# Two of the five VectorE steps of a weight conversion, given to ScalarE and GpSimd for fourteen pieces

## The chip, the core and the metric

The kernel runs on one core of one Trainium2 chip. A core has TensorE (PE in the profile, with its weight loads as PEld), VectorE (DVE), ScalarE (ACT), GpSimd (POOL) and SyncE (SP), whose queue issues most of the DMAs. Each engine works through its own queue in order, and engines wait for each other by semaphores. The metric is the device time of one execution in microseconds (us), as a median over runs.

## The reference, cut to what matters

An attention with decay runs over 4 batches, 8 heads, 768 positions and 64 channels a head. Its result, laid side by side over the heads, is x with 512 columns. Then comes a mixing by two Fourier transforms, a normalization, and two matrix products with a ReLU between them:

```python
X = np.fft.fft(np.fft.fft(x, axis=1), axis=2)
u = x + np.real(X).astype(np.float32)
un = (u - mean(u)) / np.sqrt(var(u) + 1e-06)
ch = np.maximum(un @ w_ch1, 0.0) @ w_ch2      # 512x2048 and 2048x512
return (u + ch).astype(np.float32)
```

The inputs q, k, v are float32. The two weight matrices arrive as float64, since they are float32 numbers multiplied by a float64 scalar. TensorE works on float32 here, so the kernel turns each weight, two 32-bit words in memory, into one float32.

## The kernel before, in words

The attention (`attn`, lines from 300 on) goes batch by batch, and in each batch over 6 chunks of 128 positions. A chunk loads k, q and v (L303), transposes k and q on TensorE (L314, L319), copies the transposes out of PSUM on ScalarE (kT at L316, qT at L321), and multiplies them (L338). VectorE multiplies the scores with the decay (sc, L343, two instructions a chunk, which read PSUM) and the transposed q with powers of the decay (qs, L325, which reads PSUM too). GpSimd makes the decayed k (kd, L310) and decays the running state (L362), to which VectorE adds (L363). TensorE makes the new state (L358) and the output (L373, L379), which ScalarE copies out (oT, L382) and TensorE turns back (L395). The Fourier part of a batch (`fft_ln`) begins with folds on VectorE (L476 to L571) and goes on with matrix products (L603, L615 to L620), sums and statistics (L691 to L695, L634, L635) and a normalization (L655). The `mlp` makes the two products with the weights (L749, L763). From 260 us on most of the time goes into these products, in a form that trades products for sums of quarter matrices.

The conversion of weights is `load_weights`. The weights are cut into NW = 32 word pieces of 128 partitions by 512 values. A piece comes as `raw`, 128 x 1024 words, whose even words are the low halves (`lo`) and whose odd words are the high halves (`hi`) of the numbers. Two ScalarE and five VectorE instructions make the float32:

- ScalarE L225: the sign, from the top 16 bits, as bf16, into one half of a small buffer `e`.
- VectorE L226: the exponent's bits are masked out, into the other half of `e`; ScalarE L228: they become the exponent of a bf16.
- VectorE L230: the upper mantissa with a leading one, as an integer, into the destination `w`.
- VectorE L232: the lower word scaled by 2 to the -32 and added.
- VectorE L234: exponent times sign, both bf16; VectorE L235: the mantissa, scaled, times that.

`raw` has 4 buffers (tag "hr", which the mlp uses as well), `e` has 2. In the order of pieces, two quarters of the first half of the weights (8 pieces of the first matrix, then 8 of the second) come first. A generator (`weights`) yields between pieces with a cost, and `weave` interleaves it with the attention by these costs: 8 pieces beside batch 0's attention, 6 beside batch 1's, the rest later. The framework then orders each engine's queue by its own estimates, except where `keep_in_program_order` pins an instruction. For the first two pieces (`late_words`) and for pieces 3 to 8 (`held_back`) some of the steps are pinned.

Of the kernel before, what the change touches and what calls it, by code (L numbers as in the profile page):

```python
# [11 lines left out]
F32 = mybir.dt.float32  # L12
# [4 lines left out]
AF = mybir.ActivationFunctionType  # L17
ALU = mybir.AluOpType
# [59 lines left out]
def kernel(  # L78
# [10 lines left out]
    nc = tc.nc  # L89
# [105 lines left out]
    NW = 2 * KO * DFF // WP  # L195
# [8 lines left out]
    def load_weights(dst, src):  # L204

        if src.dtype == F32:
            nc.sync.dma_start(dst, src)
            yield 1.0
            return
        raw = hp_.tile([128, 2 * WP], U32, tag="hr", name=f"raw{cnt[0]}")  # L210
        e = ep.tile([128, 2 * WP], U16, tag="e", name=f"e{cnt[0]}")
        pw, sg = e[:, 0:WP], e[:, WP:2 * WP].bitcast(BF16)
        cnt[0] += 1
        nc.sync.dma_start(raw, src.bitcast(U32))
        if LAG[0] <= landed[0] < LAG[1]:
            yield 0.5
        lo, hi = raw[:, 0:2 * WP:2], raw[:, 1:2 * WP:2]
        top = raw.bitcast(U16)[:, 3:4 * WP:4]
        d = dst.bitcast(U32)


        held_back = LAG[0] <= landed[0] < LAG[1]
        landed[0] += 1
        pin = tc.keep_in_program_order if late_words else lambda i: i
        pin(nc.scalar.activation(sg, top.bitcast(I16), AF.Sign))  # L225
        first_step = nc.vector.tensor_scalar(pw, top, 0x7FF0, None, op0=ALU.bitwise_and)  # L226
        (tc.keep_in_program_order if held_back else pin)(first_step)
        nc.scalar.activation(pw, pw, AF.Relu, bias=cvt[:, 0:1], scale=8.0)  # L228
        (tc.keep_in_program_order if held_back else pin)(
            nc.vector.tensor_scalar(d, hi, 0x000FFFFF, 0x00100000, op0=ALU.bitwise_and, op1=ALU.bitwise_or))  # L230
        del late_words[0:1]
        nc.vector.scalar_tensor_tensor(dst, lo, 2.0 ** -32, d, op0=ALU.mult, op1=ALU.add)  # L232
        p = pw.bitcast(BF16)
        nc.vector.tensor_tensor(p, p, sg, op=ALU.mult)  # L234
        nc.vector.scalar_tensor_tensor(dst, dst, 2.0 ** -20, p, op0=ALU.mult, op1=ALU.mult)  # L235
        yield 0.5 if held_back else 1.0

    late_words, landed, LAG = [0, 1], [0], (2, NW // 4)

    def weights():  # L240

        for h in range(2):
            for f in range(h * DFF // 2, (h + 1) * DFF // 2, WP):
                for c in range(KO):
                    yield from load_weights(w1[:, c, f:f + WP], w1v[:, c, f:f + WP])
            for c in range(h * FO // 2, (h + 1) * FO // 2):
                yield from load_weights(w2[:, c, :], w2v[:, c, :])
# [1172 lines left out]
```

## Time and profile before

| What | Value |
|---|---|
| median of 3 runs | 777.14 us (776.51 to 780.37) |
| profiled execution | 774.72 us, of which the span shown is 772.9 us |
| PE busy | 752.0 us, 97% |
| DVE busy | 602.9 us, 78%, 1167 instructions |
| ACT busy | 230.5 us, 30%, 532 instructions |
| POOL busy | 177.6 us, 23%, 202 instructions |
| L235, 32 instructions | median 689 ns, 658 to 1556 |
| L232, 32 instructions | median 684 ns, 671 to 694 |
| L225 and L228, 32 each | median 683 and 722 ns |

The profile is of one execution. A row of a group names the line, the engine, the operation, and what is written and read. A row of the timeline gives the start in us, the duration in us, and in brackets how long the engine had been idle before it and what ended that. Where the text says "the chain", it is the chain of work that ended last. Shares over the whole span hide the stages: the fourteen pieces of the change are converted in the first 125 us, while the attention runs.

### The profile page before, as it was taken

The numbers are of one execution on the slowest core, as the hardware profiler recorded it, in microseconds if no ns is written. First come the engines' busy times: TensorE is split into PE (matmuls) and PEld (weight loads), VectorE is DVE, ScalarE is ACT, GpSimd is POOL, SyncE is SP. The second block draws the span as 40 slices with busy tenths as digits, with TensorE's granted clock in tenths as the row PEclk, the third lists the DMA queues.
The fourth block names the chain that finished last, engine by engine and source line by source line (L and its number), as shares of the span: only waits on it lengthen the run. The fifth ranks groups of instructions, "written<-read, shape, count | busy, mean of one in ns | idle before, by whom it ended". The sixth has DMA issues, their size and how long they took to land.

```text
span 772.9 us, 14999 instructions
## 1 busy us (share of the span) xinstructions
PE 752.0 (97%) x5784; PEld 646.6 (84%) x5784; DVE 602.9 (78%) x1167; ACT 230.5 (30%) x532; POOL 177.6 (23%) x202
## 2 busy tenths in 40 slices
PE   6889999999999999999999999999999999999997
PEld 5778877767685967769846889999999999999997
DVE  6999999774936585336898999788986699758983
ACT  3755444424531221422101221034301342024310
POOL 3223330010112113220005951360015001230013
PEclk9999999999999999999999999999999999999999
DMA  9988732236843148731333465776545456455442
GB/s 236 257 176 245 202 125 94 97 93 169 249 119 95 50 82 251 185 104 40 110 68 116 153 222 158 276 233 201 185 124 178 125 180 187 125 176 179 139 140 77
DMA packets 152957, 120.23 MB, mean 156 GB/s; under 512 B 114238, under 2 KB 114622, under 8 KB 152886
## 3 DMA queue, kind: packets, MB, share of 16 engines
q1 hardware_dynamic: 145824, 100.51, 46.5%
q0 software_dynamic: 4032, 12.99, 4.9%
q10 hardware_dynamic: 3030, 5.78, 2.1%
q8 instruction: 46, 0.75, 0.4%
q14 instruction: 25, 0.20, 0.1%
HBM read 88.04 MB, written 31.20 MB: 154 GB/s over the span
## 4 chain that ended last, share of the span: by engine, by line
PE 82%; DVE 10%; DMA 3%; issue 1%; ACT 1%; SPq 1%; POOL 1%; DVEq 0%; ACTq 0%; POOLq 0%
PE p L1181 21%; PE p L1107 17%; PE pm L749 13%; PE pm L763 9%; PE p L1023 6%; PE pa L603 3%; PE pa L338 3%; PE pa L379 2%; PE pa L373 2%; PE pa L314 1%; PE pa L358 1%; PE pa L395 1%; PE pa L763 1%; DMA raw<-in_moe_w_ch_dram 1%; PE pa L319 1%
## 5 line engine op out<-in xcount | busy, mean ns | idle before, releaser
L749 PE MATMUL pm<-ut,w 128*128 128x256 f32 x512 | 118.3, 381 | 0.0
L763 PE MATMUL pm<-w,hr 128*128 128x512 f32 x240 | 109.0, 596 | 0.1
L749 PEld LDWEIGHTS pm<-ut,w 128*128 128x128 f32 x512 | 94.7, 190 | 14.4 <-issue 2.7
L763 PEld LDWEIGHTS pm<-w,hr 128*128 128x128 f32 x240 | 43.6, 190 | 44.5 <-issue 42.8
L1202 POOL TENSOR_TENSOR y<-y,u 128x512 f32<-128x512 f32 x12 | 19.9, 1662 | 186.8 <-DVE y L1211 155.5
L1181 PE MATMUL p<-tx,sx 128*128 128x128 f32 x400 | 52.7, 275 | 0.0
L1181 PEld LDWEIGHTS p<-tx,sx 128*128 128x128 f32 x400 | 48.6, 192 | 0.0
L1116 DVE TENSOR_TENSOR ha<-p,ha 128x512 f32<-128x512 f32 x60 | 39.9, 683 | 8.5 <-PE p L1107 8.3
L1187 ACT COPY y<-p 128x128 f32<-128x128 f32 x48 | 12.8, 266 | 103.6 <-PE p L1181 103.1
L310 POOL TENSOR_TENSOR kd<-k,decay 128x512 f32<-128x512 f32 x20 | 21.4, 1071 | 88.5 <-PE pa L358 47.4
L343 DVE TENSOR_TENSOR sc<-pa,decay 128x512 f32<-128x512 f32 x48 | 30.9, 682 | 12.5 <-PE pa L338 12.3
L1189 DVE TENSOR_TENSOR y<-p,y 128x128 f32<-128x128 f32 x92 | 25.5, 284 | 16.1 <-PE p L1181 9.4
L1181 PE MATMUL p<-w,ha 128*128 128x128 f32 x288 | 37.4, 275 | 0.0
L1116 DVE TENSOR_TENSOR hs<-p,hs 128x512 f32<-128x512 f32 x39 | 26.1, 683 | 12.4 <-PE p L1107 12.4
L338 PEld LDWEIGHTS pa<-qT,kT 64*128 64x128 f32 x384 | 25.1, 193 | 12.2 <-ACT qT L321 6.4
L1181 PEld LDWEIGHTS p<-w,ha 128*128 128x128 f32 x288 | 34.9, 192 | 0.1
L1107 PE MATMUL p<-sx,tx 128*128 128x128 f32 x264 | 33.9, 275 | 0.0
L757 ACT ACTIVATE hr<-pm 128x256 f32<-128x256 f32 x44 | 16.7, 383 | 57.5 <-PE pm L749 53.5
L638 POOL TENSOR_SCALAR ve<-mv 128x2 f32<-128x2 f32 x12 | 5.9, 491 | 120.1 <-DVE mv L635 120.1
L338 PE MATMUL pa<-qT,kT 64*128 64x128 f32 x384 | 30.1, 292 | 2.9 <-ACT qT L321 2.9
L1107 PEld LDWEIGHTS p<-sx,tx 128*128 128x128 f32 x264 | 31.6, 192 | 0.0
L379 PE MATMUL pa<-sc,v 128*64 128x128 f32 x384 | 28.6, 282 | 1.1 <-DVE sc L343 1.1
(274 smaller groups left out, 1747.5 us busy)
## 6 DMA issues: line engine op xcount, KB each, us to landing
tx<-td SPq DMA_DIRECT2D x84, 256.0 KB, 2.8
raw<-in_moe_w_ch_dram SPq DMA_DIRECT2D x32, 512.0 KB, 5.2
tx<-sd SPq DMA_DIRECT2D x63, 256.0 KB, 2.8
k<-in_k_dram SPq DMA_DIRECT2D x24, 256.0 KB, 5.2
q<-in_q_dram SPq DMA_DIRECT2D x24, 256.0 KB, 5.9
v<-in_v_dram SPq DMA_DIRECT2D x24, 256.0 KB, 4.9
td<-tx SPq DMA_DIRECT2D x21, 256.0 KB, 2.0
ud<-x SPq DMA_DIRECT2D x16, 256.0 KB, 2.3
```

The source lines that it names most:

```text
L310: nc.gpsimd.tensor_tensor(kd, kt, kpow, op=ALU.mult)
L338: mm(pss[hi][:, hp, :], lhsT=kT[HD[hi], hp, :], rhs=qT[HD[hi], hp, :], start=True, stop=True)
L343: nc.vector.tensor_tensor(t, pss[hi], decay[:, hi::2, :], op=ALU.mult)
L379: mm(po[HD[hi], hp, :], lhsT=vt[:, 2 * hp + hi, :], rhs=sc[hi][:, hp, :], start=(c == 0 and hp == 0), stop=(hp == HP - 1), skip_group_chec ...
L603: mm = nc.tensor.matmul(ps[:, n, :], lhsT=piece(a, i, n), rhs=cs[0:rows, a, i in (2, 3), n, :], start=(a == 0), stop=(a == 1))
L749: nc.tensor.matmul(ps, lhsT=w1[:, c, 128 * fc:128 * fc + 128], rhs=ut[:, c, :], start=(c == 0), stop=(c == KO - 1))
L763: return nc.tensor.matmul(ps, lhsT=hr[(fc - f0) // 4][:, fc % 4, 128 * i:128 * i + 128], rhs=w2[:, fc, :], start=(fc == f0), stop=(fc == f ...
L1023: nc.tensor.matmul(ps, lhsT=s2.A[a][:, kt, 128 * i:128 * i + 128], rhs=U[b][:, kt, :], start=(first and kt == 0), stop=(kt == 1), skip_gro ...
L1107: nc.tensor.matmul(ps[:, 128 * i:128 * i + 128], lhsT=ab[m][0][:, 128 * i:128 * i + 128], rhs=ab[m][1], start=(start and i == 0), stop=Tru ...
L1116: V.tensor_tensor(o, p, o, op=ADD)
L1181: nc.tensor.matmul(ps[:, 0:HM // 2], lhsT=ab[m][0][i], rhs=ab[m][1][:, i, :], start=(start and i == 0), stop=(i == HF // 2 - 1), skip_grou ...
L1189: V.tensor_tensor(o, ps[:, 0:HM // 2], o, op=ADD)
```

## The change

A new flag `shared` holds for the third to the sixteenth piece (indices 2 to 15). For them ScalarE scales the lower words by 2 to the -52 and writes them back as float32 into the places where they were read. VectorE's first sum then takes the mantissa integer, scales it by 2 to the -20 and adds the scaled lower word, in one instruction. The product with sign and exponent is left, as a plain product, to GpSimd. Exponent times sign stays on VectorE. The other 18 pieces are converted as before. The program has one VectorE instruction less, one ScalarE and one GpSimd instruction more for each of the fourteen pieces.

```diff
         held_back = LAG[0] <= landed[0] < LAG[1]
+        shared = LAG[0] <= landed[0] < NW // 2
...
-        nc.vector.scalar_tensor_tensor(dst, lo, 2.0 ** -32, d, op0=ALU.mult, op1=ALU.add)
         p = pw.bitcast(BF16)
-        nc.vector.tensor_tensor(p, p, sg, op=ALU.mult)
-        nc.vector.scalar_tensor_tensor(dst, dst, 2.0 ** -20, p, op0=ALU.mult, op1=ALU.mult)
+        if shared:
+
+            low = lo.bitcast(F32)
+            nc.scalar.activation(low, lo, AF.Copy, scale=2.0 ** -52)
+            nc.vector.scalar_tensor_tensor(dst, d, 2.0 ** -20, low, op0=ALU.mult, op1=ALU.add)
+            nc.vector.tensor_tensor(p, p, sg, op=ALU.mult)
+            nc.gpsimd.tensor_tensor(dst, dst, p, op=ALU.mult)
+        else:
+            nc.vector.scalar_tensor_tensor(dst, lo, 2.0 ** -32, d, op0=ALU.mult, op1=ALU.add)
+            nc.vector.tensor_tensor(p, p, sg, op=ALU.mult)
+            nc.vector.scalar_tensor_tensor(dst, dst, 2.0 ** -20, p, op0=ALU.mult, op1=ALU.mult)
```

## The prediction

> **What bounds the kernel now.** I read first the stretches of the span (busy time of each engine in each), because the change touches only word pieces 3 to 16, which are converted between 24 and 125 us. Columns: stretch, length, busy us (and instructions) of PE, weight load, DVE, ACT, POOL, the clock, the DMA share, GB/s.
>
> ```profile
> 20.00:30.00 10.00, 9.18 (x125) 7.68 (x123) 9.67 (x17) 8.37 (x20) 3.04 (x3) 1.00 1.04 264
> 30.00:40.00 10.00, 8.68 (x116) 7.39 (x115) 9.69 (x19) 6.26 (x15) 1.99 (x2) 1.00 1.03 251
> 40.00:50.00 10.00, 8.56 (x94) 7.23 (x94) 9.68 (x19) 8.57 (x22) 1.06 (x1) 1.00 0.98 214
> 70.00:80.00 10.00, 9.83 (x82) 8.91 (x79) 9.57 (x23) 7.32 (x16) 3.27 (x2) 1.00 0.97 267
> 80.00:90.00 10.00, 9.19 (x114) 7.78 (x114) 10.00 (x21) 4.86 (x12) 2.54 (x4) 1.00 0.59 143
> 95.00:112.00 17.00, 17.00 (x84) 14.27 (x83) 15.22 (x39) 7.43 (x19) 8.27 (x8) 1.00 0.53 174
> ```
>
> VectorE is the fullest engine until 90 us, and ScalarE is near full from 20 to 30 and 40 to 50. From 95 to 140 us TensorE has no gap (28.00 busy of 28 in the stretch after the last one shown), so nothing that VectorE saves there shows. Over 11 to 90 us the ten-microsecond stretches give TensorE 7.3 us of idle time in sum: that is all a gain can come from. Next, TensorE's instructions in order of time, whose brackets tell which engine ended each gap:
>
> ```profile
> 34.56 0.66 PE L395 MATMUL pa<-ident,ds 128*128 128x128 f32 x4 [1.32 <-ACT ds L388]
> 42.25 1.64 PE L338 MATMUL pa<-qT,kT 64*128 64x128 f32 x16 [0.52 <-ACT qT L321]
> 48.53 0.66 PE L395 MATMUL pa<-ident,ds 128*128 128x128 f32 x4 [0.92 <-ACT ds L442]
> 51.86 0.40 PE L379 MATMUL pa<-sc,v 128*64 128x128 f32 x2 [0.97 <-DVE sc L343]
> 88.59 1.09 PE L373 MATMUL pa<-qs,st 64*64 64x128 f32 x16 [0.53 <-DVE qs L325]
> ```
>
> Only two of these gaps, 0.97 and 0.53 us, are VectorE's. A third, 1.32 us, is VectorE's at one remove (ACT L228 waited 0.90 us for the mask L226, and the copy L388 was queued behind it). The others are ScalarE's own. So about 2.8 us of idle time can shrink with a faster VectorE; the other 4.5 us can't, and ScalarE gets work. Last, the collisions of VectorE and GpSimd:
>
> ```profile
> 57.11 1.06 POOL L310 TENSOR_TENSOR kd<-k,decay 128x512 f32<-128x512 f32 x1 [2.12 <-issue]
> 71.80 2.89 POOL L362 TENSOR_TENSOR st<-sd,qpow 128x256 f32<-128x256 f32 x1 [1.42 <-PE pa L379]
> 81.94 1.06 POOL L310 TENSOR_TENSOR kd<-k,decay 128x512 f32<-128x512 f32 x1 [7.25 <-PE pa L358]
> 82.30 1.24 DVE L235 SCALAR_TENSOR_TENSOR w<-w,e 128x512 f32<-128x512 f32 x1
> ```
>
> L235 takes 0.68 us alone and 1.24 beside kd: it really began at 83.54 - 0.68 = 82.86, which is 0.92 after kd did. The fold at 63.35 gives 0.94 in the same way. So a GpSimd product of this size holds VectorE up for about 0.93 us from its start. Beside the kd at 57.11 the two sc of L343, which read PSUM, took their usual 1.28: such work is not held up. The third line is the reverse: with VectorE's instructions back to back, the small product (0.67 elsewhere) needed 2.89 us and ended only after VectorE paused at 74.2.
>
> [...]
>
> **The change part by part.** I walk through the instructions as the changed program orders them. TensorE's and SP's orders are unchanged; no DMA is added, and the raw buffer is released by the instruction that stands where L232 stood.
>
> *Removed:* L235 for 14 pieces. Starts around it are 0.60 us apart (78.56 to 79.17), so 14 x 0.60 = 8.4 us of VectorE. *Replaced one for one:* L232 by the new sum, the same kind of instruction on the same shape, 0.68: nothing.
>
> *Added on ScalarE:* 14 scalings [...]mostly in its pauses, but in order ahead of copies that TensorE waits for. *Added on GpSimd:* 14 products; the kd row gives 1.06, the y row at L1202 gives 1.66 when disturbed; I take 1.06, of which 0.93 blocks VectorE unless it runs PSUM work or idles. *New wait:* the small buffer e (two of them) is released by GpSimd's product instead of L235. The mask on VectorE and the sign on ScalarE of the next piece but one wait for it, with everything queued behind them. *On GpSimd's queue* kd, the state decay L362 and the statistics stand behind products. That is covered: kd of 30.67 is used by L358 at 37.10, the decay of 32.48 at 39.48, some 6 us each.
>
> *24 to 44 us, pieces 3 to 7.* VectorE isn't what holds the chunks here: qs at 27.79 begins when ACT qT ends, and sc at 37.00 and 43.72 wait 0.24 and 0.15 us for TensorE. What VectorE saves is lost in those waits. Product by product the lock costs about 0, 0.7, 0.45, 0.74 and 0. The 1.32 us gap gets some 0.3 shorter; but piece 7's L228 is now queued ahead of kT and a scaling comes before it, which sets L338 at 42.25 back by about 0.2 from where it was. Sum +0.1, bounds -1.3 (the whole gap) and +1.0.
>
> *44 to 52 us, piece 8 and the first folds.* From sc at 43.72 to sc at 51.03 VectorE is unbroken, and TensorE waits for the latter. Less 0.60. The product starts under fold L476, and L477 waits for L476's result (48.10 follows 48.06), so GpSimd gets in there: +0.93. And the program now places two more folds, L480 (0.33) and L476 (0.60), ahead of this sc: +0.93. Sum +1.26, I take +1.2; if the product misses that slot +0.3; at best -0.75, when L338 ends (50.28). Between 52 and 62 VectorE has slack (0.65 at 54.5, 0.52 at 62.1), and the delay goes through with TensorE.
>
> *62 to 89 us, pieces 9 to 13.* VectorE is unbroken from sc at 62.14 to qs at 87.88, except for 0.36 at 74.2, and TensorE waits for that qs. Less 4 x 0.60 = 2.4 (piece 13's L235 stood behind qs). Piece 13's L234 comes ahead of it: +0.34. Piece 11's mask is placed right behind piece 10's and needs piece 9's product, which is queued behind the decay of 71.80 that starves: VectorE stops for 0.5 + 0.95, of which 0.36 it lost before: +1.1. Products of pieces 10 and 12 fall among masks: 2 x 0.93. Piece 11's falls beside sc: 0. Piece 13's beside L691 and L692, which read PSUM: +0.3. Sum -2.4 + 0.34 + 1.1 + 1.86 + 0.3 = +1.2; bounds -0.5 (the idle time to be had) and +2.5.
>
> *After 95 us.* Pieces 14 to 16 lie beside a gapless TensorE: 0, which costs up to 1 us if GpSimd gets the statistics out late.
>
> Sum: 0.1 + 1.2 + 1.2 = +2.5 us. On the profiled execution's own 774.72 us (span 772.9) that is 777.2. The median of the runs shown, 777.14, lies 2.4 above that execution; added to the median it is 779.6, which I predict.
>
> **The rivals.**
> *Faster.* The products mostly fall beside PSUM work and idle moments, and VectorE's 97% is the true bound. Then the three gaps go (1.32 + 0.97 + 0.53 = 2.8), and with less head-of-line waiting on ScalarE some more, up to the 7.3 us: 774.3, at the extreme 769.8. For it speaks the busy share; against it, that VectorE waits for others at each chunk until 44 us and that the kd collisions are no rarity.
> *Clearly slower.* One mechanism: the lock costs more than it saves. If all 14 products meet SBUF work, each costs 0.93 - 0.60 = 0.33, 4.6 us; with the two folds ahead of sc (0.93) and the stop for piece 11 (0.5 beyond the lock) that is +6.0: 783.1. It takes the lead where the mean block exceeds 0.60 us also from 24 to 44 us, so that sc stops waiting for TensorE there. My walk has a mean of 0.54 over the first 11 products.
> *Nothing.* The chunks go at the pace of TensorE, ScalarE and the loads (DMA share 0.98 to 1.04 from 20 to 50 us), and what moves on VectorE is absorbed: 777.1 within 1 us.
>
> **How the numbers follow.** Chances: the forecast 0.35 (its own range 777.5 to 781.5), faster 0.33, clearly slower 0.22, nothing 0.10. About 0.5%, 3.9 us, is what a measurement of this kernel can tell from no change. Of faster, 0.20 lies beyond it, since that needs more than the three gaps; of the slower cases 0.22 + 0.06. The rest, 0.52, is within. The range runs from 772.0 (5.1 us of the 7.3) to 783.5 (just past the slower rival); about 0.1 is left out on either side.
>
> **What would show it.** In the changed profile: L235's rows down from 32 to 18; VectorE's mask, sum and fold rows with mean durations up by some tenths; the product on GpSimd at 1.1 to 1.4; sc of the second sequence's first chunk near 52.3 in place of 51.03; a VectorE gap ended by POOL before a mask near 75; qs later than 87.88 by about 2.5. If sc there starts before 51 us, or VectorE's rows stay at their means, I am wrong.

## The result, and the profile after

The changed kernel takes 787.62 us (median of 6 runs, 785.02 to 792.56), the kernel before 777.44 us (6 runs, 775.66 to 780.37). The ratio is 1.0134, with a 95% interval from 1.0114 to 1.0153: 10.2 us slower, where 2.5 us slower had been forecast, and outside the range. The profiled execution took 786.97 us, its span is 785.2 us against 772.9.

The busy times are the first surprise. Part 1 of the page of after:

```profile
PE 754.4 (96%) x5784; PEld 647.5 (82%) x5784; DVE 603.5 (77%) x1153; ACT 238.3 (30%) x546; POOL 196.4 (25%) x216
```

VectorE has 14 instructions fewer and is as busy as before (602.9 us). What was taken away came back as collisions: an instruction that is kept out by GpSimd counts as busy while it waits (the fold L486 below is busy for 1.53 us beside a product instead of 0.69; E15 to E18 separate the two). The groups of after on VectorE, shapes kept apart (busy us, mean ns | idle before):

```profile
L227 DVE TENSOR_SCALAR e<-raw 128x512 uint16<-128x512 uint16 x32 | 17.9, 558 | 7.1 <-DMA raw<-in_moe_w_ch_dram 5.5 <-POOL w L240 1.6
L231 DVE TENSOR_SCALAR w<-raw 128x512 uint32<-128x512 uint32 x32 | 16.0, 501 | 0.0
L238 DVE SCALAR_TENSOR_TENSOR w<-w,raw 128x512 f32<-128x512 uint32 x14 | 10.9, 775 | 0.7 <-ACT raw L237 0.2
```

The same three steps had means of 461, 444 and 685 ns before. Lines from 245 on of before are 9 further down in after; the sign L225 is L226, the mask L226 is L227, the exponent L228 is L229, the relu of the mlp L757 is L766, sc L343 is L352, qs L325 is L334. The files of the experiments have line numbers of their own; there the names of the tiles tell what a row is.

TensorE, which up to 140 us had only two waits for VectorE of more than 0.2 us, 0.97 and 0.53 us, has longer ones now. TensorE's rows of after with the large waits:

```profile
54.86 0.40 PE L388 MATMUL pa<-sc,v 128*64 128x128 f32 x2 [2.08 <-DVE sc L352]
...
95.88 1.09 PE L382 MATMUL pa<-qs,st 64*64 64x128 f32 x16 [1.95 <-DVE qs L334]
...
142.15 3.66 PE L758 MATMUL pm<-ut,w 128*128 128x256 f32 x8 [2.40 <-ACT hr L766]
```

The first two answer to the waits of 0.97 and 0.53 us at 51.86 and 88.59 of before. The third has no counterpart: before, TensorE had no gap from 95 to 140 us. And its eight matmuls take 3.66 us, where eight of this kind take 1.89 elsewhere in the trace. The stretches of after show why (the clock is the third column from the right):

```profile
140.00:142.00 2.00, 0.00 (x0) 0.00 (x0) 1.50 (x4) 1.45 (x3) 0.00 (x0) 1.00 0.67 233
142.00:144.00 2.00, 1.85 (x5) 1.50 (x6) 2.00 (x6) 0.86 (x3) 0.00 (x0) 0.58 0.07 29
144.00:146.00 2.00, 2.00 (x8) 1.64 (x7) 2.00 (x6) 1.60 (x5) 0.00 (x0) 0.57 0.39 111
```

After the idle time TensorE's granted clock is at half for some 3.4 us (0.65, 0.50, 0.50 and 0.64 in the four microseconds from 142 us on).

The way the delay builds up is best seen from the starts of the same TensorE step in both traces, since TensorE's order is the same. Worked out as after less before; E1, E4, E13 and E16 are experiments below (an offset of up to some 2 us comes from the loads at 27 us, which differ from execution to execution: TensorE waits 1.78 us for one in E1 and 2.34 in E13):

| TensorE step, start before | after | E1 | E4 | E13 | E16 |
|---|---|---|---|---|---|
| L338 at 27.87 | +1.26 | +1.25 | +1.24 | +2.24 | +0.44 |
| L338 at 49.12 | +1.88 | +1.09 | +1.40 | +1.93 | -0.04 |
| L338 at 55.19 | +3.00 | +1.34 | +2.52 | +4.21 | -0.46 |
| L338 at 60.95 | +3.34 | +1.34 | +2.86 | +4.75 | -0.46 |
| L338 at 86.90 | +5.87 | +1.75 | +5.12 | +4.74 | +0.00 |
| L373 (qs) at 88.59 | +7.29 | +3.28 | +7.37 | +6.91 | -0.40 |
| L660 (un) at 92.08 | +7.30 | +3.28 | +8.95 | +8.44 | -0.39 |
| L660 at 150.53 | +11.65 | +4.27 | +9.49 | +8.44 | -0.39 |

Three stages lose: 49 to 61 us, 61 to 92 us, and 121 to 150 us. In the first, VectorE's rows of after show both predicted losses, the collision and the two folds that now stand ahead of sc:

```profile
49.33 1.53 DVE L486 TENSOR_TENSOR fo<-fo,xn 128x512 f32<-128x512 f32 x1
...
53.10 0.41 DVE L489 TENSOR_TENSOR fo<-fo 65x255 f32<-65x255 f32 x1
53.43 0.68 DVE L485 TENSOR_TENSOR fe<-x,x 128x512 f32<-128x512 f32 x1
54.03 1.28 DVE L352 TENSOR_TENSOR sc<-pa,decay 128x512 f32<-128x512 f32 x2
```

L486 takes 1.53 instead of 0.69 us beside a product, and sc begins at 54.03 instead of 51.03. In the second stage VectorE's rows of after have the predicted stop of piece 11's mask for GpSimd:

```profile
79.32 0.43 DVE L227 TENSOR_SCALAR e<-raw 128x512 uint16<-128x512 uint16 x1 [1.64 <-POOL w L240]
```

The third stage shows at ScalarE. Its rows of after:

```profile
132.58 0.57 ACT L673 COPY ut<-pa 128x512 f32<-128x512 f32 x1
137.93 0.70 ACT L226 ACTIVATE e<-raw 128x512 bf16<-128x512 int16 x1 [4.79 <-DMA raw<-in_moe_w_ch_dram]
138.50 0.74 ACT L229 ACTIVATE e<-e,cvt 128x512 uint16<-128x512 uint16 x1
140.55 0.67 ACT L226 ACTIVATE e<-raw 128x512 bf16<-128x512 int16 x1 [1.31 <-DMA raw<-in_moe_w_ch_dram]
141.12 0.70 ACT L229 ACTIVATE e<-e,cvt 128x512 uint16<-128x512 uint16 x1
141.74 0.36 ACT L766 ACTIVATE hr<-pm 128x256 f32<-128x256 f32 x1
```

The relu for which TensorE waits is queued behind two pieces (the 18th and 19th) that wait for their loads. These pieces are not among the fourteen. Before, this relu stood behind the sign of the first, which didn't wait for its load, and ahead of the sign of the second, which did. The change doesn't touch it: the scheduler, which orders each engine's queue, placed it otherwise once the instructions around it were others. ScalarE's order alone doesn't make this wait: in E14, which has it with VectorE's order of before, the delay is 6.12 us at the step before this one and 6.13 us behind it.

### The profile page after: what moved, and what is told of

Same layout as the page of the kernel before. It is cut to its first block, busy times and chain, and to the rows that moved or that the text cites. A ratio compares the mean times of both kernels' runs of the same rounds, so it can differ in the third digit from the quotient of the medians.

```text
span 785.2 us, 15030 instructions
## 1 busy us (share of the span) xinstructions
PE 754.4 (96%) x5784; PEld 647.5 (82%) x5784; DVE 603.5 (77%) x1153; ACT 238.3 (30%) x546; POOL 196.4 (25%) x216
## 4 chain that ended last, share of the span: by engine, by line
PE 81%; DVE 10%; DMA 4%; ACT 2%; issue 2%; POOL 1%; SPq 1%; DVEq 0%; ACTq 0%; POOLq 0%
PE p L1190 21%; PE p L1116 17%; PE pm L758 12%; PE pm L772 9%; PE p L1032 6%; PE pa L347 3%; PE pa L388 2%; PE pa L612 2%; PE pa L382 2%; DMA raw<-in_moe_w_ch_dram 2%; PE pa L323 1%; PE pa L367 1%; PE pa L404 1%; DMA q<-in_q_dram 1%; PE pa L328 1%
## 5 line engine op out<-in xcount | busy, mean ns | idle before, releaser
L758 PE MATMUL pm<-ut,w 128*128 128x256 f32 x512 | 120.1, 385 | 2.4 <-ACT hr L766 2.4
L352 DVE TENSOR_TENSOR sc<-pa,decay 128x512 f32<-128x512 f32 x48 | 30.9, 682 | 13.1 <-PE pa L347 13.1
L766 ACT ACTIVATE hr<-pm 128x256 f32<-128x256 f32 x44 | 16.8, 384 | 56.9 <-PE pm L758 54.0
```

Source lines behind the costliest of these rows:

```text
L352: nc.vector.tensor_tensor(t, pss[hi], decay[:, hi::2, :], op=ALU.mult)
L758: nc.tensor.matmul(ps, lhsT=w1[:, c, 128 * fc:128 * fc + 128], rhs=ut[:, c, :], start=(c == 0), stop=(c == KO - 1))
```

## The experiments

Three theories were to be told apart. The lock: GpSimd's products exclude VectorE, as forecast, only more of it. ScalarE: the scalings stand ahead of copies that TensorE waits for. The order: the loss comes from where the scheduler put other instructions, not from the work that was moved.

The summary first; "V" and "S" are the orders of VectorE's and ScalarE's other instructions. Ratios are to before, run on the same chip beside each kernel; medians of different rows can come from different chips, so the text compares ratios.

| | work | order | median us | ratio, 95% interval |
|---|---|---|---|---|
| after | both | new V, new S | 787.62 | 1.0134 (1.0114 to 1.0153) |
| E1 | both | old V, old S | 780.48 | 1.0043 (1.0030 to 1.0056) |
| E2 | scaling | old V, old S | 777.10 | 1.0001 (0.9989 to 1.0014) |
| E3 | product | old V, old S | 780.40 | 1.0040 (1.0025 to 1.0056) |
| E4 | both | new V, old S | 785.49 | 1.0102 (1.0074 to 1.0129) |
| E5 | both | old V, new S | 781.26 | 1.0070 (1.0048 to 1.0093) |
| E6 | none | V of after | 782.79 | 1.0101 (1.0074 to 1.0128) |
| E7 | none | S of after | 780.87 | 1.0077 (1.0051 to 1.0104) |
| E8 | product, pieces 9 to 16 | old V, old S | 778.97 | 1.0029 (1.0011 to 1.0047) |
| E9 | both | after, hr moved | 785.79 | 1.0118 (1.0093 to 1.0143) |
| E10 | both | after, qs moved | 787.25 | 1.0139 (1.0108 to 1.0171) |
| E11 | both | E1, qs moved | 779.93 | 1.0034 (1.0019 to 1.0049) |
| E12 | none | before, qs moved | 776.75 | 1.0001 (0.9986 to 1.0016) |
| E13 | none | V of after, old S | 781.45 | 1.0075 (1.0037 to 1.0114) |
| E14 | none | old V, S of after | 781.31 | 1.0051 (1.0036 to 1.0066) |
| E15 | no product at all | old V, old S | 775.10 | 0.9973 (0.9964 to 0.9983) |
| E16 | memset of w for it | old V, old S | 774.68 | 0.9970 (0.9952 to 0.9988) |
| E17 | square of w for it | old V, old S | 779.56 | 1.0030 (1.0009 to 1.0051) |
| E18 | memset of e for it | old V, old S | 775.21 | 0.9986 (0.9972 to 1.0000) |

### Work and order apart: E1 to E5

An order is held by an edge, without a semaphore, from each instruction of an engine to the next one in the wanted order; added instructions are left free.

```diff
+    for x, y in zip(line, line[1:]):
+        tc.add_manual_dep(y, x.name, mybir.DependencyInfo(
+            mybir.DependencyClass.NoSync, mybir.DependencyReason.DATA), reason="as_before")
```

E1 is the change with VectorE's and ScalarE's orders of before.

> The change's work whole (14 scalings on ScalarE, 14 products on GpSimd), but ScalarE's and VectorE's other instructions stand in the order that they had before the change. The order theory (the loss comes from what the scheduler rearranged: relu hr behind two pieces' loads at 137 us, two folds ahead of sc) expects within 3 us of before, 777 to 780. The lock theory (GpSimd's products hold VectorE up) expects 782 to 785: only the 4.35 us at 137 to 142 us and some 1 us for the folds come back. The ScalarE theory (the scalings are in the way of copies that TensorE waits for) expects the same total, but with gaps ended by ScalarE copies, not by sc and qs.

E1 is 0.43% over before, some 3.3 us, of after's 1.34%. So two thirds of the loss are order, and the order theory's number is met. What is left sits where the lock theory has it. TensorE's two large waits in E1:

```profile
53.20 0.40 PE L482 MATMUL pa<-sc,v 128*64 128x128 f32 x2 [1.22 <-DVE sc L446]
...
91.87 1.09 PE L476 MATMUL pa<-qs,st 64*64 64x128 f32 x16 [2.05 <-DVE qs L428]
```

The first is the 0.97 us of before with 0.25 on it, not 2.08 as in after: the two folds no longer stand ahead. The second has grown by 1.5 us although nothing new stands ahead of qs.

E2 keeps the scaling on ScalarE and leaves the product to VectorE:

```diff
-            nc.gpsimd.tensor_tensor(dst, dst, p, op=ALU.mult)
+            nc.vector.tensor_tensor(dst, dst, p, op=ALU.mult)
```

> Only the scaling on ScalarE; the last product stays on VectorE, so VectorE does as many instructions as before and GpSimd no more than before; orders as before the change. The ScalarE theory expects 780 to 783 (3 us or more over before). The lock theory expects 777 to 778.5: ScalarE has pauses. The order theory expects 777 to 778.

The ratio is 1.0001. The ScalarE theory falls: fourteen scalings of 0.69 us (median of the row in after) cost nothing that can be measured in this order.

E3 moves the product alone; the factor goes into the bias of the exponent's conversion:

```diff
-        nc.scalar.activation(pw, pw, AF.Relu, bias=cvt[:, 0:1], scale=8.0)
+        nc.scalar.activation(pw, pw, AF.Relu, bias=(cvt20 if shared else cvt)[:, 0:1], scale=8.0)
...
-        nc.vector.scalar_tensor_tensor(dst, dst, 2.0 ** -20, p, op0=ALU.mult, op1=ALU.mult)
+            nc.gpsimd.tensor_tensor(dst, dst, p, op=ALU.mult)
```

> Only the last product on GpSimd; the lower word is scaled where it was before, inside VectorE's sum (the factor 2^-20 goes into the bias of the power's conversion, which costs no instruction); orders as before the change. The lock theory expects 780 to 784: most of the loss of E1 is here. The ScalarE theory expects 774 to 777, since VectorE does 14 instructions fewer. The order theory expects about 777.

E3 costs what E1 costs (1.0040 and 1.0043). As far as can be measured, all that the work itself loses is the product's.

E4 holds only ScalarE's order, E5 only VectorE's; the other is left to the scheduler, which puts some of its instructions otherwise than in after.

> The change with only ScalarE's other instructions in the order that they had before; VectorE's order is left to the scheduler. All theories expect the 4.35 us at 137 to 142 us to come back (relu hr ahead of the pieces that wait for loads): 782 to 784. If it stays at 787, that wait wasn't what cost the time there. The difference from E1 is what VectorE's new order costs: about 1 us by the walk (two folds ahead of sc), 3 or more by the order theory.

> The change's work whole, VectorE's other instructions in the order from before, ScalarE's left to the scheduler: the corner that E1, E4 and after lack. If the two orders add up, it is E1's 780.5 plus the 2.1 us between E4 (785.5) and after (787.6): 782.6. If ScalarE's order costs the whole 4.35 us that the trace of after shows at 137 to 142 us (relu hr behind two pieces that wait for loads) wherever VectorE stands: 784.8. If the wait at 137 appears only because VectorE's new order had made everything late, 780.5.

E4 gives back 0.32% of after's 1.34%, about 2.5 us, and not the 4.35 that the trace shows at 137 us. From E1 to E4, VectorE's order costs 0.59%, 4.6 us; by the other way round, from E5 to after, 0.64%. ScalarE's order costs 0.27% (E1 to E5) or 0.32% (E4 to after). Work 0.43, VectorE's order 0.6, ScalarE's 0.3: that they add up to 1.34 is no test, since they are differences along one path. Each difference is uncertain by about 0.3, so VectorE's is clear of noise and ScalarE's hardly is.

### The order alone, with nothing moved: E6, E7, E13, E14

E6 has the instructions of before, VectorE's first 190 (to about 130 us) in after's order, each last product right behind its factors. E7 has those of before with ScalarE's in after's order. The edit is the same loop over another list.

> Before's work (nothing on GpSimd or ScalarE added), but VectorE's first 190 instructions in the order that the scheduler gave them in after, each last product right behind its two factors. The order theory expects +5 us as between E1 and E4: 782. The theory that order and product cost together (the mask of piece 11 right behind that of piece 10 waits for GpSimd's product of piece 9, which no order of before has to wait for) expects only the folds placed ahead of sc, 0.9 to 1.3 us: 778.

> Before's work with ScalarE's instructions in the order of after (without the scalings, which aren't there): relu hr stands behind two pieces whose loads land at 138 to 141 us. If this order alone makes the wait and the fall of TensorE's granted clock after it, +4.35 us: 781. If it only does so with the delays of the changed work, 777.

Both are as slow as the order theory said or slower. But other instructions had moved beside them: in E6 some of ScalarE's and one load, in E7 some of VectorE's, with sc ahead of qs. So both were run again with all else held.

> E6 again without what moved beside it: before's work, VectorE's first 190 instructions in after's order, ScalarE's and SP's in before's. If VectorE's order alone costs what E6 showed: 782 to 783. If E6's cost came from ScalarE's order and the swapped load that moved beside it: 778 (the folds ahead of sc alone).

> E7 again without what moved beside it (in E7 VectorE's sc had come ahead of qs): before's work, ScalarE's instructions in after's order, VectorE's in before's. If ScalarE's order alone costs as much as with the work (E5 less E1, 2 us): 779. If nothing of E7 is left: 777.

E13 is 0.75% over before and E14 0.51%. With not one instruction more on GpSimd or ScalarE, VectorE's order, with the products where E13 puts them, alone costs 5.8 us (2.9 to 8.9), ScalarE's 4.0 (2.8 to 5.1). The expectation that E6's cost was ScalarE's order and the load, with only the folds left in E13, is refuted, and E14 costs more than the difference of E5 and E1, so the parts do not add up from this side. Why is not shown. None of E14's loss is the relu at 137 us. In its trace TensorE loses 2.85 us while its clock is at half for 6.8 us, from the end of a wait of 2.03 us (at 36.35; 1.32 us in before). TensorE's rows of E13:

```profile
54.73 0.41 PE L479 MATMUL pa<-sc,v 128*64 128x128 f32 x2 [1.90 <-DVE sc L443]
...
95.50 1.09 PE L473 MATMUL pa<-qs,st 64*64 64x128 f32 x16 [2.69 <-DVE qs L425]
```

The first wait is 0.93 longer than in before, the two folds to the hundredth. Ahead of qs now stand piece 13's exponent times sign and its product. VectorE's rows of E13:

```profile
90.45 0.42 DVE L305 TENSOR_TENSOR e<-e 128x512 bf16<-128x512 bf16 x1
90.90 0.69 DVE L306 SCALAR_TENSOR_TENSOR w<-w,e 128x512 f32<-128x512 f32 x1
```

Before, these two followed qs (89.72 and 90.37 against 87.88). They take 1.06 us from 90.45 to the next start at 91.51, of the 2.16 by which the wait grew. Another 0.55 us is the mantissa step at 88.96, which takes 0.84 us instead of 0.41 and overlaps the one instruction that GpSimd has from 88 to 91 us (0.52 us; by its place and length the memset of sd, 0.53 us in before and after). The product at 90.90, 0.61 of the 1.06 us, stands ahead of qs only because E13 has it right behind its factors; in after it is on GpSimd. So E13 is VectorE's order of after with fourteen products that this run placed itself.

### Why the product costs: E8, E15 to E18

E8 is E3 with the product moved for pieces 9 to 16 only.

```diff
-        shared = LAG[0] <= landed[0] < NW // 2
+        shared = NW // 4 <= landed[0] < NW // 2
```

> E3 with only pieces 9 to 16 on GpSimd; pieces 3 to 8 keep their last product on VectorE. E3's trace loses 0.1 us from 28 to 61 us and about 3.8 us from 67 to 95 us, so: 780 (all of E3's 3.5 us). If the products of pieces 3 to 8 cost as much each as the others, 6 of 14 go: 778.9. If it was the lock as my prediction sized it by stage (+1.2 for each of the two stages), 778.6.

It has 0.29% of E3's 0.40%; the intervals overlap, so it supports, without showing, that pieces 3 to 8 cost little.

E15 leaves the products out altogether. E16 to E18 put something else in their place on GpSimd:

```diff
-            nc.gpsimd.tensor_tensor(dst, dst, p, op=ALU.mult)
+            nc.gpsimd.memset(dst, 0.5)
```

E17 has `nc.gpsimd.tensor_tensor(dst, dst, dst, op=ALU.mult)` there, and E18 `nc.gpsimd.memset(p, 1.0)`.

> E3 with the 14 products left out altogether, on VectorE and on GpSimd (so the weights of pieces 3 to 16 are left without their exponents); orders as before. It tells what taking 14 instructions of 0.60 us off VectorE is worth where they stood. My prediction's terms (0.6 us at piece 8, 0.5 us of idle time that can go before 89 us) give 775.5 to 776. If VectorE's 97% was the true bound: 774 or less. The difference from E3's 780.4 is what the products cost on GpSimd.

> E3 with GpSimd's product replaced by a memset of the same piece, which reads nothing (so the product is left out of the result); it stands at the same places of GpSimd's queue, waits for the same sum and holds the same kd, decays and statistics behind it for some 0.5 us instead of 1.16. If the cost of E3 is the exclusion of VectorE while GpSimd reads SBUF, it goes: as E15, within 0.5 us. If it is what stands behind the product on GpSimd's queue, about half of it stays: 778. If a memset excludes VectorE as well, 778 to 780.

> E3 with GpSimd multiplying the sum by itself in place of the signed power (so the factor is left out of the result): it reads SBUF as long as the product does, but no longer holds the small buffer e, so no mask or sign waits for GpSimd. If the exclusion is the cost: as E3, 779.5 to 780.5. If the wait for e is: as E16, 775.

> E3 with GpSimd's product replaced by a memset of the small buffer e (so the product is left out of the result): it reads nothing, but the masks and signs of the next piece but one wait for it as for the product, queued at the same places on GpSimd. If the wait for e is the cost: near E3, 779 or more. If the exclusion is: near E16, 775 to 776.

The four make a table of two by two, with E3: reads SBUF and holds e (E3) 1.0040, reads and doesn't hold (E17) 1.0030, holds and doesn't read (E18) 0.9986, neither (E16) 0.9970. Reading costs 0.54% with the wait and 0.60% without, 4.2 to 4.7 us (uncertain by 0.2 and 0.3%); the wait for e costs 0.10 to 0.16%, which these intervals can't tell from nothing. GpSimd's queue is not the cost: E16 has as many instructions in it as E3 and is as fast as E15, which has no product. Its memsets are also shorter (0.53 us, against 1.16 for the product and 1.15 for E17's square), but if the time on GpSimd were the cost, about half should stay, and nothing does. VectorE's busy time says the same without the noise of the medians. Part 1 of the pages of E15, E16, E17 and E3:

```profile
PE 751.5 (97%) x5784; PEld 646.0 (83%) x5784; DVE 595.3 (77%) x1153; ACT 230.4 (30%) x532; POOL 176.2 (23%) x203
PE 751.4 (97%) x5784; PEld 645.7 (84%) x5784; DVE 596.1 (77%) x1153; ACT 230.5 (30%) x532; POOL 184.0 (24%) x217
PE 751.7 (97%) x5784; PEld 646.0 (83%) x5784; DVE 602.9 (78%) x1153; ACT 230.5 (30%) x532; POOL 192.9 (25%) x217
PE 753.5 (97%) x5784; PEld 647.1 (83%) x5784; DVE 603.5 (78%) x1153; ACT 230.6 (30%) x532; POOL 193.7 (25%) x217
```

All four have VectorE's same 1153 instructions. Where GpSimd reads SBUF (E17, E3), VectorE is busy for about 7 to 9 us longer than where it has nothing to do (E15) or only writes (E16, and E18 with 594.8). In these runs what reads is also what multiplies; which of the two holds VectorE up, they do not tell apart. E16's TensorE rows where before waited 0.53 us and E1 2.05:

```profile
86.90 1.16 PE L441 MATMUL pa<-qT,kT 64*128 64x128 f32 x16 [0.29 <-ACT qT L424]
88.19 1.09 PE L476 MATMUL pa<-qs,st 64*64 64x128 f32 x16
```

The wait for qs is gone. E15 says what taking the products off VectorE could have won in this order: 2.1 us (0.27%) for 14 instructions less. On GpSimd they then cost 0.67% (E3 less E15), 5.2 us, that is 0.37 us each.

### Single moves: E9 to E12

E9 and E10 take after's order for both engines and move one instruction; E11 does to E1, and E12 to before, what E10 does to after.

```diff
-    L226 L229 L226 L229 hr
+    hr L226 L229 L226 L229
```

> After with one instruction moved on ScalarE: the relu hr for which TensorE waits at 142.15 us stands ahead of the two pieces whose loads land at 137.9 and 140.6 us, not behind them; all else in after's order. If that place costs what after's trace shows (2.40 us of waiting and 1.8 us for the half-speed clock behind it), 787.6 - 4.2 = 783.4. If the clock falls anyway or the wait only moves, 785 to 787.6. If the loss is GpSimd's and ScalarE's added work itself, 787.6.

TensorE's rows of E9 at the place:

```profile
138.28 2.79 PE L705 MATMUL pa<-cs,fe 128*128 128x193 f32 x16
140.90 1.89 PE L851 MATMUL pm<-ut,w 128*128 128x256 f32 x8
```

The gap of 2.40 us is gone and the eight matmuls take 1.89 us again. In the trace the delay from 92 to 150 us is 0.01 us (8.61 to 8.62), where it was 4.35. In the medians it is 0.16%, with intervals that overlap. Of the difference, the trace of E9 explains 0.64 us: at 162.25 TensorE waits 1.57 us for un, 0.99 at that step in after. So what the trace of after shows at this place is the cost in that execution, and what it costs in the median is not shown.

```diff
-    x BN_STATS BN_STATS AGGREGATE qs
+    qs x BN_STATS BN_STATS AGGREGATE
```

> After with one instruction moved on VectorE: qs of the chunk at 92.8 us stands ahead of the second half of x (L704), the two BN_STATS and an aggregate, not behind them; all else in after's order. TensorE waits 1.95 us for it in after's trace: 785.6 if nothing else is late next, 784.5 or less if the clock that falls in some executions behind such a gap no longer does. If sc or the statistics on GpSimd are late next: 787.

> E1 (the change's work in the orders from before) with the same single move of qs. In E1's trace TensorE waits 2.05 us for qs against 0.53 in before. The clock theory (a gap of about 2 us also makes TensorE's clock fall to half for about 4 us in most executions: E1's mean clock is 0.998 or less in 13 of 20, before's in 16 of 55) expects nearly all of E1's 3.6 us back: 777 to 777.5, with mean clocks like those of before. Only the wait: 778.8. The lock theory (the products cost everywhere): 780.

> Before with qs moved ahead of one BN_STATS and one aggregate, nothing else. TensorE's wait for qs in before's trace is 0.53 us: 776.4 against 776.9. If the executions of before with a low mean clock (16 of 55, some 2 us slower) have it from this gap, a little more, 776. If un, which needs the statistics, is late next: no difference.

None of the three gains anything that can be measured, as the last theory of each expectation had it (E12 moves qs ahead of one BN_STATS and one aggregate only). E10's trace has no wait for qs there any more, but this:

```profile
99.03 0.43 PE L481 MATMUL pa<-sc,v 128*64 128x128 f32 x2 [1.50 <-DVE sc L445]
```

The wait has moved to the next thing that VectorE owes. In E12 it is 0.25 and 0.16 us for sc. This speaks for VectorE's backlog as a whole, and against the place of one instruction in it; and no version with the products made was found that beats the kernel before.

## Why the prediction was wrong

**The lock was right, and so was the sign, but two thirds of the loss is something else.** The new order of VectorE and ScalarE costs 0.91% (after less E1), some 7 us; the sum had 1.3 us for it (0.93 and 0.34). Without these two terms it had 1.2 us for the work itself; E1 measures 3.3. On the path it had 4.2 us of lock (0.93 + 1.1 + 1.86 + 0.3), and E3 less E15 is 5.2. It had 3.0 us of saving ("Less 0.60", "Less 4 x 0.60"), and E15 measures 2.1 for all fourteen. Of the 5.2 us, 1.6 are TensorE's slower clock by the reckoning below (a mean of 2.3 us in E3, 0.7 in E15), for which the sum had no term. "Mostly in its pauses", for the scalings, was right (E2). The sign was no safe forecast: it gave "faster" 0.33, and each stage's bounds reached below zero.

**24 to 44 us, +0.1:** right. From 27.87 to 42.25 after loses 0.62 and E1 gains 0.16.

**44 to 52 us, +1.2:** right, by its parts. After loses 1.12 from 49.12 to 55.19, E1, without the folds, 0.25; "two more folds ahead of this sc: +0.93" is what E13's wait shows.

**62 to 89 us, +1.2, bounds -0.5 and +2.5:** this is the first step that failed. After loses 3.96 from 60.95 to 92.08, E1 1.94. The signs named are there: the stop for piece 11 (1.64 us), the collisions. The step followed VectorE to qs alone, and there after's wait has grown by 1.42 us. Two waits for ScalarE's copy oT, which the step put at nothing, lose 1.13 and 1.06 us more: one of 1.61 us at 70.75 (0.48 before), behind a sign that waits for its load and a scaling, and one of 0.91 us at 91.80 (none before). The second comes through VectorE:

```profile
88.40 1.72 DVE L227 TENSOR_SCALAR e<-raw 128x512 uint16<-128x512 uint16 x1
90.16 0.72 ACT L229 ACTIVATE e<-e,cvt 128x512 uint16<-128x512 uint16 x1 [3.43 <-DVE e L227]
91.80 0.66 PE L404 MATMUL pa<-ident,oT 128*128 128x128 f32 x4 [0.91 <-ACT oT L391]
```

The mask takes 1.72 us instead of 0.42 beside a product (88.22, 1.16 us) and a memset (89.32, 0.53 us) on GpSimd, the exponent waits for the mask, and oT is queued behind the exponent. The step also priced one displaced instruction ("Piece 13's L234 comes ahead of it: +0.34") and took the rest of the order as it was. E13, which has no product on GpSimd, loses 3.69 us there, and the table says where: nothing up to 86.90, 2.17 in the wait for qs, 1.53 in the half-speed clock behind that wait.

**After 95 us, "Pieces 14 to 16 lie beside a gapless TensorE: 0":** the second step that failed, by 4.35 us in this execution; in the median its cost is not clear of noise (E9). The step looked at the fourteen pieces alone and not at what the scheduler does to instructions behind them. The order of the changed program was known before the run, and relu hr stood behind the signs of two later pieces in it. In E1, with the old order, the 0.99 us from 92 to 150 stay within the "up to 1 us" that the step allowed.

**Every wait was priced at its length**, in the sum and in the rivals ("1.32 + 0.97 + 0.53 = 2.8"). This is the third step that failed: a wait of TensorE of 1.9 us and more cost more than its length in most cases. In the 20 profiles there are 18 falls of TensorE's clock to half between 14 and 170 us. Each lasts 3.4 us (one of them 6.8), with a clock of 0.50 in the full microseconds inside it, and so costs 1.7 us of full-speed time (3.4). Sixteen come with a wait of TensorE of 1.90 to 2.94 us, two with a pair of waits, 1.5 to 1.6 and 0.40 us, close together. Eight waits of 1.90 to 2.33 us have no fall (2.08 and 1.95 in after, 2.05 in E1, 2.24 in E17 among them), and single waits below 1.9 us (the longest 1.88, in E6) have none. Over all runs, the mean clock's deficit times the span is about 4 us in after, 0.9 in before (its runs beside the experiments), 2.0 in E1, 3.8 in E13 and 3.5 in E14. So the clock would be about 3 of after's 10.2 us, 2.8 of E13's 5.8 and 2.5 of E14's 4.0. This is a reckoning from recorded clocks, not an experiment. After's spread goes with it: its runs go from 785.02 us at a mean clock of 0.999 to 792.56 at 0.990. Why the clock fell behind some of the waits of 1.90 to 2.33 us and not behind others, no run shows.

**The rivals.** "Faster" asked that products fall beside PSUM work; with no product on GpSimd (E15, E16) the time in before's order is 0.997 of before's, 775 of 777.14, so that rival's 774.3 was about its end, and 769.8 was out of reach. "Clearly slower" had the right mechanism for the work and ended at 783.1; it lacked most of the order, and the clock. A rival that the order alone makes the loss was missing.

**The signs named ahead.** The rows of L235 (L244 in after) are 18. The product's row is 1.15 to 1.65 us, median 1.16. Mask, mantissa and sum are longer by 0.06 to 0.10 us in the mean, less than "some tenths". sc begins at 54.03 against the "near 52.3", of which 1.88 us is delay from before this stage. The gap ended by GpSimd is at 79.32, not near 75. qs begins at 95.17, against 87.88 + 2.5.

Open: some 0.5 of the 2.16 us by which the wait for qs grows in E13; whether the wait for e costs anything; what the relu at 142 us costs in the median; and how much of each loss by order would stay if the clock didn't fall.

## What to carry to other kernels

Where a scheduler orders the queues, compare the whole order of every engine before and after an edit, not only the edited instructions: here twice as much was lost to what moved (0.91%) as to what was changed (0.43%). Take work off a full engine only to a place that doesn't block it: a product on GpSimd that reads SBUF cost VectorE's path more (5.2 us) than its removal was worth (2.1), while fourteen instructions on ScalarE cost nothing measurable in the old order (E2, ratio 1.0001). Follow a held-up instruction to the engine that waits for it, and to what is queued behind that. And price a wait of TensorE of about 2 us above its length: here 16 of 24 waits of 1.90 us or more came with a clock of 0.50 for 3.4 us (6.8 in one case), which is 1.7 us of full-speed time (3.4).

## What the runs showed of the hardware that was not expected

- TensorE's clock fell to 0.50 for 3.4 us (6.8 in E14) with 16 of 24 waits of 1.90 us or more (up to 2.94 us), and not with the other eight.
- A memset of 128 x 512 on GpSimd (0.53 us), in place of each product, cost nothing that could be measured beside a VectorE busy for 77% of the span (E16 0.9970, E15 without it 0.9973), a multiplication of the same size (1.15 us) 0.6% (E17, 1.0030). In one place VectorE was held up beside what is by its length a memset all the same: the mantissa step at 88.96 in E13 took 0.84 us instead of 0.41.
- VectorE's busy time stayed at 603 us with 14 instructions fewer, and fell to 595 to 596 us when GpSimd read nothing in their place: an instruction that is kept out counts as busy (L486 in after, 1.53 us instead of 0.69).
